# Pairs of tokens for k, a shorter end of MoE2, and a new written-out order in an attention and two-MoE kernel

## The chip, the cores and the metric

One core of one Trainium2 chip runs the whole program in one launch. The metric is the device time of one execution in microseconds (us). The kernel before ran three times: 928.71, 931.66 and 931.54 us, median 931.54. Durations are taken from one more execution, the profiled one.

## The reference

```python
scores = scale * np.matmul(q, k.transpose(0, 1, 3, 2))        # B, H, S, D = 4, 8, 576, 64
bias = -(cum[:, :, :, None] - cum[:, :, None, :])             # cum = cumsum of max(s, 0)
scores = np.where(causal, -1e9, scores + np.minimum(bias, 0.0))
attn = softmax(scores)
x = np.matmul(attn, v)                                        # to 2304 x 512
h = x @ moe_w_in                                              # 512 x 2048
x = (h - np.tanh(h)) @ moe_w_out
out = ((x @ moe2_w_a) * (x @ moe2_w_b)) @ moe2_w_out          # d_ff 1536
```

The inputs are fp32. The kernel makes most products from fp16 pieces: a value is a high and a low half, and a product takes three matmuls.

## The kernel before, in words

**Attention.** The work is cut into units, each a pair of heads of one batch (`Unit`, L968). A first-half unit has the first two tiles of 128 tokens as queries and two tiles of keys (`nk` = 2); a second-half unit (`merged`) has the rest. There are 16 of each. `g_load` (L993) loads q, k and v for a group of 2 or 4 units. A second-half group already reads the first two tiles of k and v as pairs of tokens: a row of 512 bytes holds tokens 2p and 2p+1, so that tile 0 has the even tokens and tile 1 the odd ones. For its queries all those keys are allowed, so their order does not matter. A first-half group reads each tile on its own, in rows of 256 bytes. `g_scale` and `split` scale q and k and cut them into fp16 halves (`qk`), `u_turn` (L1107) has the DMA queue transpose them to `qkT` and copies parts to `qB` and `kB`, whose extra rows hold the bias (`u_load`, from a DRAM buffer that `bias_parts`, L1796, fills). `u_qk` (L1139) then makes, for each head and query tile t, two matmuls over (t+1) x 128 key columns, and DVE adds the causal mask. Softmax, transposes and the product with v follow.

**MoE1 and MoE2.** Each block of tokens goes through MoE1 and MoE2. The last blocks use a scheme with seven products for four (`seven`, L1548, operands `ghl`), and the output product is treated in the same way (`four_act`, L1639, and `four_mm`, L1661, operands `sq`). `four_act` makes the operands of two halves of the tokens; those of the second half (l = 1) go to DRAM (`pb_d`) and are read back into a tile `x2f` when `four_mm` needs them. For the last two pieces of the last block's second half the output product is plain and sums up in two PSUM banks of its own, `blk["plain"]`. `four_out` (L1710) copies sums from PSUM (e into the one buffer "th", f into one of two "g"), combines them into `ob` and scales the rows by y1 and y2 (`out_rows`, L1729); `plain_out` (L1701) adds the plain sums, and `out_store` (L1738) issues the store, on SP or ACT for the last 512 rows.

**The order.** All operations are recorded first, so that the profile has one line, L647, for all of them, and an operation is told by its tiles. Then `emit` (L452) writes them out in the order that the string `ORDER` (L37) holds: three characters are one step, an operation's number and, where several engines may do it, the choice. `follow` (L445) uses the string if its length fits the number of operations. `cost` (L684) holds the durations by which a planner would set an order; with a fitting string it decides nothing. Tiles of a pool come free in this order too, so a tile with one buffer ties its users together.

```python
            for m, (qs, ks) in enumerate(u.pairs):
                pl.tensor.matmul(
                    pq[:, :n * P], qs[:, qat(u, h, t), :],
                    ks[:, h * u.wk:h * u.wk + n, :].rearrange("p a c -> p (a c)"),
                    start=(m == 0), stop=(m == 1))
```

Of the kernel before, what the change touches and what calls it, by code (L numbers as in the profile page):

```python
# [41 lines left out]
    "AFNAFgAMYAQIAGUAGgAQMAGkAKJAGoAHgAHkAG9APcAPkAYUAh0AHoAPsAGuAPgAH8AP0AGwAHAAHuAG0AZIAHEAh8AKBAHwAG5AHIAKQAKUAKYAKcAKgAH0"
    "AKkAJmAIAALQAFkAMuAM1AKoAQgALcAIEAP4AIIAYYAiQAKsAKyAM6AM8ALBAH5ALEAP8ALIAXwAK0ALgANIAJpALUALYALkANAARAANEAQwARQAlcAYcANM"
    "ANQALMAX0AX4AX8ALoAYgALsALyAK4AYAAK8AMBANUAYEAZQAL0AMEAIMANYANeAIRANtAN8AL4AL9AYIANwAOAAMIAiMAOIANhAUQAPoANkAYOAMMAiIAN0"
    "AYkAOEAjIAiUAOMAOQANpAiYAicAUYAikAigAOUAQkAN4AioAixAOYAMQAOeAOtAisAYoATwAOwAO0Ai9AOgAOkAQoAMVAlqAT4AO5AOoAO8AliAjAAQsAjV"
    "AjYAPAAlkAT8AT0AZcAjcAjMAjEAlsAl0AlxAUAAUEAQ0AYsAQ4AjRAUUAjgAZgAZkAi0AZoAYQAQ8ARgAZwAUcAUgAREAUkAUIAUMAUwAaAAZ0AYyAi4ARI"
    "An8AY0AZUARMAakAjlAaEAaIAU4AU8AjqAU0AVAAkgAj4ARwAjsAaMAaUAaYAZsAaoASgARVAoAAUsARYAjwAqSAj0Aj8AkAAl4Al8AasAksAn2AkkAawARl"
    "ARoARcAn4AZYAoIARsASAAqUAR1AkEAVEAkoAbIAqKAoGAZ4AUoAVQAVUAkwAR4AVYAVcAkIAk0AbMAbsASwAa4ASkAkMAnwAmAAmEAVMAVIAa8AZ8AR8AkU"
    "AbQAVgAqMAVwAk4AkQAadAmIAoNAk8AbwAagAbUAV4AbCAkYAb0AbYAcQASEAmMAV0AlIAlAAVkAmQAV8AWAASoAnAAnEAbcAmUAcUAcYASIAnIAqcAa0AoS"
    "AlFAzMAlMAbgAkcAbEAmYAb4AccASQAVsAmcAb8Am0AckAcAAqaAmgAm4Am8AcEAcoAlQAzYAS0AS4AblAzQAzUAzgAoUASMAboAc0AnMASUAmkAmpAoYAnQ"  # L50
    "AnUAcKAzcAWEAVoAcMAocAnYAlUAlYASYApIAc4AWMAndAmsAcuAc8AngAzkAdAAaQAqiApUA5MAdIApMAogApQAzoAdMAScAdYAWIAWQAmwAnkAWUAqmApY"
    "AokApcAooASsAdcAcwATAApgAdgAosAzsApkAS8ApoApxAowAdkAdQAptAWYAWcAzwAqoAqsAz0Ap0Ao8Ao2AdUApAAdsAWwAW4ATQAnoAntAp4Aq0AWgArc"
    "AdwAWkAW8Aq4Ad8AeAAqwAo5ApEAroAeEArgAegAd2Az4Ad4ATEAq8ArABEoAz8A0AArEAWoATIArQArKArsArwBEwArkAdoAekAeoAW0ATMAXAA0kArMAWs"
    "Ar0Ap8A0EAeIATUA0JAXEA0yAXIAr4AeQA0MA0qA24Ar8AsBAcgArUAsEATYAesA0YA28AXMAeUA3EAqAA0cATgAsIA00A0sATcAXQAXUAXYAXcAfoAfEAeZ"
    "A3IAecATlA3AA0gAToATsA3OA06AXgAsMArYA08AsQAsUAsYA5QAgMA5YAfsAfwAfIAdEAf0A0QA1EAewAfMAXkAscAf4AsgA3QAskA1CA3YAf8BE8AXsBEs"
    "AssA1IBE0A7kBE4AgQA7sA18Ae0AgwAfQAswAsoAfYA3UAs1As4A1UAtgAtoAtsAuIAe4Ag0A0UAtkAtBAgUAtFAfUAeMA1MAgYA5dAgcAtIA2AA1QAg4A1Y"
    "A5UAfcA2EA1cAg8As8A3cA5kA1gAgAA3oAe8A7wAtMAuMA1kAtQAhAA7oA1oAtUA3gBFQBFIAuQAtwA3sA1tAtZAhIAt0AXoAfAAggA3wAt4AfiA3kAt8AuU"
# [92 lines left out]
    "EXsEYQEVkEXZEXwEXcEYgEY0EY8EYkEXiEY5EZIEZMEbUEZQEYcEZUEbMEbcEbIEYVEYZEbYEZBEXkEZYEZ9EbQEbgEVoEZcEZlEZtEZxEZpEZhEZ0EZ4EaB"  # L150
    "EX4EX8EX0EbkEbsEboEbwEb0EaIEb4EaMEb8EaZEcAEaVEcsEcwEc0EaQEaEEc4Ec8EdAEacEahEapEasEakEa1Ea4EawEa8EbAEcEEcNEcIEcREcZEcgEcU"
    "EccEcoEdYEdcEdhEclEdIEdNEdQ"
# [1895 lines left out]
```

## Time and profile before

| | |
|---|---|
| median of three runs | 931.54 us |
| the profiled execution | 930.71 us |
| its span, first to last instruction | 928.9 us |
| PE, DVE, ACT, POOL busy | 881.3, 805.7, 574.1, 346.1 us |
| instructions | 20616 |
| moved by DMA | 123.38 MB |
| mean granted TensorE clock | 0.995 |

PE is the engine for matmuls, PEld its weight loads, DVE, ACT and POOL the vector, scalar and GpSimd engines; SP only issues DMAs (SPq, and ACTq for those that ACT issues). The busy times are sums over the whole span, for PE 95% of it. They don't tell in which stretch an engine waits, so the rows below come from windows and timelines.

### The profile page before, as it was taken

To read this page: it belongs to the slowest core of one execution; us is meant where nothing else is said; L and a number is where in the kernel's file an instruction comes from. 1 tells how busy PE (TensorE), PEld (TensorE's weight loads), DVE (VectorE), ACT (ScalarE), POOL (GpSimd) and SP (SyncE) were. 2 spreads that over 40 slices of the span, in tenths; PEclk is the share of its full clock that TensorE was granted. 3 is DMA by queue.
4 is the path that set the end of the run, shared out by engine and by line. 5 is a ranking of instruction groups with operands and counts; after the bars stand their busy time and mean duration, and the time that the engine had idled before them with its cause. 6 is when DMAs were issued, how large, how long until landed. Compare 5 with 4: busy or idle time off the path is not lost.

```text
span 928.9 us, 20616 instructions
## 1 busy us (share of the span) xinstructions
PE 881.3 (95%) x7650; PEld 647.6 (70%) x7650; DVE 805.7 (87%) x2011; ACT 574.1 (62%) x1136; POOL 346.1 (37%) x495
## 2 busy tenths in 40 slices
...
GB/s 204 304 214 238 231 123 124 113 154 171 206 165 174 193 179 167 208 137 161 308 206 189 84 24 1 69 2 1 47 54 53 60 185 65 62 72 112 72 68 115
DMA packets 260197, 123.38 MB, mean 133 GB/s; under 512 B 228544, under 2 KB 236976, under 8 KB 260096
## 3 DMA queue, kind: packets, MB, share of 16 engines
...
q8 instruction: 60, 0.98, 0.4%
q14 instruction: 41, 0.34, 0.1%
...
## 4 chain that ended last, share of the span: by engine, by line
PE 47%; DVE 5%; issue 2%; DMA 1%; POOL 1%; ACT 0%; SPq 0%; POOLq 0%; DVEq 0%; ACTq 0%
PE h L647 16%; PE qk L647 12%; PE acc L647 11%; PE pv L647 8%; DVE w L647 1%; DVE x2f L647 1%; DVE g L647 1%; DMA x2f<-pb_d 0%; DMA out_dram<-x2f 0%; DVE a L647 0%; DVE ghl L647 0%; DVE sq L647 0%; DVE xf L647 0%; DVE h L647 0%; DVE th L647 0%
## 5 line engine op out<-in xcount | busy, mean ns | idle before, releaser
L647 PEld LDWEIGHTS <-w 128*128 128x128 f16 x3840 | 372.2, 98 | 67.0 <-issue 4.0
L647 PE MATMUL h<-xhl,w 128*128 128x256 f16 x2256 | 276.9, 273 | 2.4 <-DVE ghl L647 1.1
L647 PE MATMUL acc<-w,ghl 128*128 128x512 f16 (+1 forms) x1092 | 233.6, 358 | 0.9 <-DVE sq L647 0.9
L647 PEld LDWEIGHTS <-ghl 128*128 128x128 f16 x1290 | 123.6, 98 | 99.9 <-issue 4.8
L647 PE MATMUL h<-xf,w 128*128 128x256 f16 (+1 forms) x416 | 71.3, 310 | 0.0
L647 DVE CUSTOM_DVE_ANT_0 qk<-qk,caus,cs 128x384 f32<-128x384 f32 (+3 forms) x120 | 64.9, 555 | 2.8 <-PE qk L647 1.4
L647 PE MATMUL qk<-xf,w 128*128 128x256 f16 x432 | 55.2, 273 | 0.8 <-DVE xf L647 0.6
L647 PE MATMUL pv<-xf,w 128*128 128x256 f16 x432 | 55.0, 273 | 0.0
L647 ACT ACTIVATE g<-h 128x512 f32<-128x512 f32 x40 | 23.4, 592 | 48.8 <-PE h L647 27.0
L647 ACT ACTIVATE w<-w 128x1024 f32<-128x1024 f32 (+1 forms) x45 | 50.9, 1156 | 1.4 <-DVE w L647 1.4
L647 ACT ACTIVATE th<-h,xc 128x512 f32<-128x512 f32 x64 | 43.7, 683 | 9.5 <-PE h L647 7.4
L647 PE MATMUL qk<-qkT 128*128 128x128 f16 (+4 forms) x168 | 45.7, 316 | 3.7 <-ACT zs L647 3.1
L647 PE MATMUL qk<-kB,qB 67*128 67x128 f16 (+4 forms) x168 | 45.3, 313 | 3.9 <-ACT zs L647 2.2
L647 PEld LDWEIGHTS <-v 128*64 128x64 f16 x1440 | 37.7, 113 | 12.8 <-issue 10.8
L647 PEld LDWEIGHTS <-x2f 128*128 128x128 f16 x360 | 35.1, 98 | 7.1 <-DMA x2f<-pb_d 0.8
L647 DVE SCALAR_TENSOR_TENSOR h<-h,xc,th 128x512 f32<-128x512 f32 x48 | 36.0, 751 | 1.6 <-ACT th L647 1.6
L647 ACT ACTIVATE zs<-qk,nm 128x128 f32<-128x128 f32 (+1 forms) x64 | 30.2, 472 | 11.2 <-DVE nm L647 9.4
L647 DVE SCALAR_TENSOR_TENSOR ghl<-h,xsg,ghl 128x512 f16<-128x512 f32 x48 | 35.8, 746 | 1.4 <-ACT ghl L647 0.9
L647 DVE SCALAR_TENSOR_TENSOR a<-qk,sm,a 128x512 f16<-128x512 f32 (+1 forms) x56 | 35.2, 630 | 1.4 <-ACT a L647 1.0
L647 ACT ACTIVATE qk<-qk,nm 128x512 f32<-128x512 f32 (+1 forms) x56 | 31.7, 566 | 7.4 <-DVE nm L647 5.4
L647 ACT ACTIVATE sq<-qk 128x512 f32<-128x512 f32 x22 | 13.1, 594 | 37.4 <-PE qk L647 35.0
L647 PE MATMUL pv<-aT,v 128*64 128x128 f16 x960 | 34.5, 225 | 1.3 <-DVE aT L647 0.8
...
## 6 DMA issues: line engine op xcount, KB each, us to landing
...
```

The source lines that it names most:

```text
L647: return getattr(getattr(plan.nc, name), what)(*[real(a) for a in args], **{k: real(a) for k, a in kw.items()})
```

## The change

Five things change.

1. `g_load`: a first-half group reads k as pairs of tokens, one DMA in rows of 512 bytes in place of two in rows of 256 (five k loads in place of ten). `bias_parts` lays the first half's bias out in the same way.
2. `u_qk`: a first-half unit's products read k by stepping between the two tiles, so that the columns of the result are in the order of tokens again. Neighbouring elements of the moving operand are 256 bytes apart. Number and size of the matmuls stay: 64 of 128 and 64 of 256 columns.
3. `four_act` and `four_mm`: the last piece of the last block stays in its tile `sq4`; the store to `pb_d` and the load from it are left out.
4. `four_out` for the last block's second half (`own`): e and f use a part of the weight tile `w1`, and the rows are scaled by a product yy of y1 and y2, on any of three engines.
5. `cost` has other DMA rates, and `ORDER` is another string, for 4562 steps in place of 4569.

```diff
@@ -35,121 +35,121 @@
 ORDER = (
-    "AAMAAEAB0AAIAAQAAUAAAAAYABsAB4ABoABwAAcAAgAAkAAsAAwAA0ABEABJABNABSAAoAA4AA8ABAABVABZABkACEACAAB8ACIACMACQACYAQQAIkACUACc"
...
+    "AAMABwAAIABsAB0AAAABkAAEABoAAQAAUACAAAYAB8AB4AAcAAgAAkAAsAAwAA0AQIABEABJABNABRAIgABUABYAAoAA4ACEACIACMAA8ACUAIcAIQABAACQ"
...
@@ -701,9 +701,9 @@
         size = {F32: 4, I32: 4}.get(main.dtype, 2)
         b = rows * count(main) * size
         if what == "dma_start_transpose":
-            return 650.0, 1600.0, b / 220.0
+            return 650.0, 1600.0, b / 242.0
         hold = 475.0 if b < 2e4 else 636.0 if b < 9e5 else 560.0
-        return hold, 910.0 if b < 1e6 else 2000.0, b / (180.0 if main.shape[-1] * size < 512 else 360.0)
+        return hold, 910.0 if b < 1e6 else 2000.0, b / (150.0 if main.shape[-1] * size < 512 else 360.0 if b >= 1e6 else 300.0)
     if eng == "tensor":
         lhs = rd[0]
         rate = 4.0 if lhs.dtype == F32 else 1.0
@@ -1013,6 +1013,11 @@
                 pl.sync.dma_start(
                     t.rearrange("p (h t) d -> p h (t d)", t=w)[:, :, 0:far * D],
                     heads[:, 0:far * P, :].rearrange("h (p t) d -> p h (t d)", t=far))
+            if nm == "k" and not u.merged:
+                pl.sync.dma_start(
+                    t.rearrange("p (h t) d -> p h (t d)", t=w),
+                    heads[:, 0:nt * P, :].rearrange("h (p t) d -> p h (t d)", t=nt))
+                far = nt
             for x in range(far, nt):
                 pl.sync.dma_start(
                     t.rearrange("p (h t) d -> p t h d", t=w)[:, x],
@@ -1143,10 +1148,11 @@
         pl.hold = (u.a[h],)
         with pl.group():
             for m, (qs, ks) in enumerate(u.pairs):
-                pl.tensor.matmul(
-                    pq[:, :n * P], qs[:, qat(u, h, t), :],
-                    ks[:, h * u.wk:h * u.wk + n, :].rearrange("p a c -> p (a c)"),
-                    start=(m == 0), stop=(m == 1))
+                o, r = pq[:, :n * P], ks[:, h * u.wk:h * u.wk + n, :].rearrange("p a c -> p (a c)")
+                if not u.merged:
+                    r = ks[:, h * u.wk:h * u.wk + u.nk, 0:n * P // u.nk].rearrange("p a c -> p c a")
+                    o = o.rearrange("p (c a) -> p c a", a=u.nk)
+                pl.tensor.matmul(o, qs[:, qat(u, h, t), :], r, start=(m == 0), stop=(m == 1))
         c = col(u, h, t)
         pl.vector.tensor_tensor_reduce(
             out=pq[:, :n * P], in0=pq[:, :n * P], in1=caus[:, (NT - t) * P:],
@@ -1655,6 +1661,8 @@
                 copy_scaled(o[:, 0, to], x, 1.0)
                 lo_part(o[:, 1, to], x, 1.0, o[:, 0, to])
             res.append(o)
+        if many(blk, c) == 4 and c == C2 - 1:
+            return res
         pl.sync.dma_start(pb_d[(blk["nth"] - FOUR) * C2 + c][:, 0:2 * many(blk, c) * P], t, writes=[("pb", blk["nth"], c)])
         return res
 
@@ -1666,7 +1674,7 @@
             else:
                 blk["acc", l] = accs(4)
         o = blk["p", c][l]
-        if l:
+        if l and not (plain(blk, c) and c == C2 - 1):
             t = new("moe", [P, 1024], I32, "x2f", 2, True).bitcast(F16)[:, 0:2 * many(blk, c) * P]
             pl.sync.dma_start(t, pb_d[(blk["nth"] - FOUR) * C2 + c][:, 0:2 * many(blk, c) * P], reads=[("pb", blk["nth"], c)])
             o = t.rearrange("p (h s n) -> p h s n", h=2, n=P)
@@ -1701,16 +1709,19 @@
     def plain_out(blk, ob):
         for i in (1, 0):
             g = blk["off"] // P + 3 - i
-            yy = new("moe", [P, 1], F32, "wac", 3)
-            small("tensor_tensor", out=yy, in0=y1[:, g:g + 1], in1=y2[:, g:g + 1], op=ALU.mult)
+            yy = blk["yy", i]
             r = ob[:, i * 512:(i + 1) * 512]
             pl.vector.scalar_tensor_tensor(out=r, in0=blk["plain"][i], scalar=yy, in1=r, op0=ALU.mult, op1=ALU.add)
             out_store(g, r)
 
     def four_out(blk, l):
         z, y1_, y2_, x = blk["acc", l]
-        e = new("moe", [P, 512], F32, "th", 1, True)
-        f = new("moe", [P, 512], F32, "g", 2, True)
+        own = l and plain(blk, C2 - 1)
+        if own:
+            e, f = [w1[:, 14, i * 512:(i + 1) * 512].bitcast(F32) for i in range(2)]
+        else:
+            e = new("moe", [P, 512], F32, "th", 1, True)
+            f = new("moe", [P, 512], F32, "g", 2, True)
         ob = new("moe", [P, 1024], I32, "x2f", 2, True).bitcast(F32)
         copy_scaled(e, z, 1.0, True)
         copy_scaled(f, y1_, 1.0, True)
@@ -1723,17 +1734,22 @@
         pl.vector.tensor_tensor(out=ob[:, 0:256], in0=x[:, 0:256], in1=e[:, 0:256], op=ALU.add)
         for i in (1, 0):
             r = ob[:, i * 512:(i + 1) * 512]
-            out_rows(blk["off"] // P + 2 * l + 1 - i, r, r, not (l and plain(blk, C2 - 1)))
+            if own:
+                g = blk["off"] // P + 3 - i
+                blk["yy", i] = new("moe", [P, 1], F32, "wac", 3)
+                small("tensor_tensor", out=blk["yy", i], in0=y1[:, g:g + 1], in1=y2[:, g:g + 1], op=ALU.mult)
+                copy_scaled(r, r, blk["yy", i])
+                continue
+            out_rows(blk["off"] // P + 2 * l + 1 - i, r, r)
         return ob
 
-    def out_rows(g, ob, src, store=True):
+    def out_rows(g, ob, src):
         kw = dict(out=ob, in0=src, scalar1=y1[:, g:g + 1], scalar2=y2[:, g:g + 1], op0=ALU.mult, op1=ALU.mult)
         if src is ob:
             small("tensor_scalar", **kw)
         else:
             pl.vector.tensor_scalar(**kw)
-        if store:
-            out_store(g, ob)
+        out_store(g, ob)
 
     def out_store(g, ob):
         for p0, n, row in where[g]:
@@ -1799,10 +1815,10 @@
         R = B * H
         d = x[:R, 0:w].bitcast(F32)
         x = x[:R, w:w + 3 * w // 2].bitcast(F16).rearrange("p (k w) -> p k w", k=3)
-        far = FAR * P if w == S else 0
+        far = FAR * P
         for o, c in ((d, cr[:, 0:w]),) if not far else (
                 (d[:, 0:far].rearrange("p (t c) -> p t c", t=FAR), cr[:, 0:far].rearrange("p (c t) -> p t c", t=FAR)),
-                (d[:, far:w], cr[:, far:w])):
+                (d[:, far:w], cr[:, far:w]))[:1 + (w > far)]:
             pl.vector.tensor_scalar(
                 out=o, in0=c, scalar1=cr[:, base:base + 1], scalar2=sig[:R], op0=ALU.subtract, op1=ALU.mult)
         for i in range(3):
```

Three places in the order of the instructions follow. The number at the end of a tile's name tells instances apart.

SP at the start, from the first MoE1 weights (w1) to the first two DMA transposes. Here ws is raw q, k and v of the second group of two units (the first group's loads are ahead), part0_d the bias in DRAM. Before:

```order
L647 DMA w1_0_154<-in_moe_w_in_dram 128x4x512
L647 DMA ws_1_156<-in_v_dram 128x4x64 x2
L647 DMA part0_d_71<-x2f_0_124 48x1x256
L647 DMA ws_1_156<-in_q_dram 128x4x64 x2
L647 DMA ws_1_156<-in_k_dram 128x4x64 x2
L647 DMA part0_d_71<-x2f_0_124 48x1x256
L647 DMA_TRANSPOSE qkT_0_200<-qk_0_165 128x8x128
L647 DMA_TRANSPOSE qkT_1_204<-qk_1_163 128x8x128
```

And now:

```order
L647 DMA w1_0_131<-in_moe_w_in_dram 128x4x512
L647 DMA ws_1_138<-in_v_dram 128x4x64 x2
L647 DMA ws_1_138<-in_q_dram 128x4x64
L647 DMA part0_d_71<-x2f_0_133 48x1x256
L647 DMA ws_1_138<-in_q_dram 128x4x64
L647 DMA ws_1_138<-in_k_dram 128x4x128
L647 DMA part0_d_71<-x2f_0_133 48x1x256
L647 DMA_TRANSPOSE qkT_0_190<-qk_0_170 128x8x128
L647 DMA_TRANSPOSE qkT_1_196<-qk_1_164 128x8x128
```

The group's two k loads are one, and the second tile of q is issued behind the first bias store.

DVE at the start, from the second bias step to the scaled sum of squares p2n (x2f: the bias here; icap and cap: limits of the scales). Before:

```order
L647 TENSOR_TENSOR x2f_0_124<-x2f_0_124 32x256
L647 TENSOR_SCALAR icap_0_129<-p2a_0_117 128x1
L647 TENSOR_SCALAR cap_0_131<-sig_0_121 128x1
L647 TENSOR_SCALAR icap_0_129<-icap_0_129 128x1
L647 TENSOR_SCALAR icap14_0_134<-icap_0_129 128x1
L647 TENSOR_TENSOR x2f_0_124<-x2f_0_124 32x256
L647 TENSOR_SCALAR x2f_0_124<-x2f_0_124 32x256
L647 TENSOR_SCALAR p2n_1_148<-pv_1_146 128x3
```

And now:

```order
L647 TENSOR_TENSOR x2f_0_133<-x2f_0_133 32x256
L647 TENSOR_SCALAR x2f_0_133<-x2f_0_133 32x256
L647 TENSOR_SCALAR icap_0_142<-p2a_0_124 128x1
L647 TENSOR_SCALAR cap_0_144<-sig_0_128 128x1
L647 TENSOR_SCALAR p2n_1_148<-pv_1_146 128x3
```

One TENSOR_TENSOR on the bias is gone from DVE here, and two of the four small steps come behind p2n.

DVE at the end, to its last instruction (x2f_26: the last block's first half; x2f_31: its second half; the last two rows add the plain products). Before:

```order
L647 TENSOR_TENSOR g_92_13063<-g_92_13063,th_92_13074 128x512
L647 TENSOR_TENSOR x2f_26_13117<-qk_222_12488,g_92_13063 128x512
L647 TENSOR_TENSOR x2f_26_13117<-qk_223_12489,th_92_13074 128x256
L647 TENSOR_SCALAR x2f_26_13117<-x2f_26_13117,y1_0_1749,y2_0_8637 128x512
L647 TENSOR_TENSOR th_93_13127<-th_93_13127 128x256
L647 TENSOR_TENSOR x2f_31_13132<-g_93_13130 128x256
L647 TENSOR_TENSOR g_93_13130<-g_93_13130,th_93_13127 128x512
L647 TENSOR_TENSOR x2f_31_13132<-qk_234_12955,th_93_13127 128x256
L647 TENSOR_TENSOR x2f_31_13132<-pv_142_12954,g_93_13130 128x512
L647 TENSOR_SCALAR x2f_31_13132<-x2f_31_13132,y1_0_1749,y2_0_8637 128x512
L647 SCALAR_TENSOR_TENSOR x2f_31_13132<-acc0_20_13085,wac_36_8639,x2f_31_13132 128x512
L647 SCALAR_TENSOR_TENSOR x2f_31_13132<-acc1_20_13078,wac_35_8641,x2f_31_13132 128x512
```

And now:

```order
L647 TENSOR_TENSOR th_92_13063<-th_92_13063 128x256
L647 TENSOR_TENSOR x2f_31_13084<-qk_234_12927,w1_0_131 128x256
L647 TENSOR_TENSOR x2f_31_13084<-x2f_31_13084,w1_0_131 128x256
L647 TENSOR_TENSOR x2f_31_13084<-pv_142_12926,w1_0_131 128x512
L647 TENSOR_TENSOR g_92_13066<-g_92_13066,th_92_13063 128x512
L647 TENSOR_TENSOR x2f_26_13109<-x2f_26_13109,th_92_13063 128x256
L647 TENSOR_TENSOR x2f_26_13109<-qk_222_12491,g_92_13066 128x512
L647 TENSOR_SCALAR x2f_26_13109<-x2f_26_13109,y1_0_1772,y2_0_8608 128x512
L647 TENSOR_TENSOR x2f_26_13109<-qk_223_12492,th_92_13063 128x256
L647 TENSOR_SCALAR x2f_26_13109<-x2f_26_13109,y1_0_1772,y2_0_8608 128x512
L647 SCALAR_TENSOR_TENSOR x2f_31_13084<-acc0_20_13070,wac_36_8877,x2f_31_13084 128x512
L647 SCALAR_TENSOR_TENSOR x2f_31_13084<-acc1_20_13077,wac_35_8677,x2f_31_13084 128x512
```

The four sums of x2f_31 have moved ahead of the last of x2f_26, and its scalings are gone from DVE, to ACT and POOL.

## Rows read from the trace of the kernel before

**Rows 1.** Stages: us, busy time of PE, PEld, DVE, ACT, POOL, PEclk, DMA share, GB/s

```profile
0.00:17.00 17.00, 0.49 (x3) 0.41 (x4) 12.91 (x47) 9.88 (x20) 3.29 (x13) 1.00 0.80 189
17.00:45.00 28.00, 19.41 (x144) 12.61 (x144) 26.32 (x113) 26.70 (x69) 14.95 (x28) 1.00 1.05 293
45.00:170.00 125.00, 118.61 (x801) 78.18 (x799) 120.63 (x388) 116.01 (x257) 51.54 (x94) 0.99 0.83 179
170.00:430.00 260.00, 257.66 (x2685) 170.46 (x2685) 234.86 (x657) 207.24 (x417) 124.43 (x174) 1.00 0.90 171
430.00:475.00 45.00, 41.17 (x349) 27.82 (x348) 41.03 (x96) 39.45 (x56) 9.91 (x14) 1.00 0.70 246
475.00:920.50 445.50, 444.00 (x3676) 358.15 (x3674) 365.87 (x710) 174.81 (x320) 140.49 (x171) 1.00 0.24 74
```

**Rows 2.** Timeline of the start: start, us busy, engine, line, operation, tiles

```profile
9.36 0.14 DVE L647 TENSOR_SCALAR p2n<-pv 128x3 f32<-128x3 f32 x1
...
10.78 0.88 DVE L647 SCALAR_TENSOR_TENSOR qk<-ws,sc,qk 128x256 f16<-128x256 f32 x2
...
11.43 1.05 SPq L647 DMA_DIRECT2D ws<-in_k_dram  x2
...
13.22 2.81 SPq L647 DMA_TRANSPOSE qkT<-qk  x2
...
17.38 0.27 PE L647 MATMUL qk<-qkT 128*128 128x128 f16 x1
```

**Rows 3.** Two windows of the start: rows of 256 bytes arrive, then long rows

```profile
2.00:5.00 3.00, 0.00 (x0) 0.00 (x0) 1.16 (x2) 0.00 (x0) 0.98 (x4) 1.00 0.92 198
7.00:9.00 2.00, 0.16 (x1) 0.00 (x0) 1.80 (x8) 1.45 (x6) 0.40 (x1) 1.00 1.03 376
```

**Rows 4.** PE timeline in 17 to 45, at 63 and at 150 us; qkT alone

```profile
18.40 0.42 PE L647 MATMUL acc<-qkT 128*128 128x256 f16 x1
...
18.61 0.42 PE L647 MATMUL acc<-kB,qB 67*128 67x256 f16 x1
...
63.33 3.62 PE L647 MATMUL h<-xf,w 128*128 128x256 f32 x16
...
150.39 0.27 PE L647 MATMUL qk<-qkT 128*128 128x256 f16 x1
...
150.50 0.27 PE L647 MATMUL qk<-kB,qB 67*128 67x256 f16 x1
...
17.00:45.00 28.00, 5.50 (x16) 2.19 (x16) 0.96 (x3) 1.23 (x2) 1.85 (x3) 1.00 1.05 293
```

**Rows 5.** Timeline of the end, and the group of scalings on DVE

```profile
908.65 0.69 DVE L647 SCALAR_TENSOR_TENSOR ghl<-xtail,ghl 128x512 f16<-128x512 f32 x1 [0.78 <-ACT ghl L647]
...
910.51 0.82 PE L647 MATMUL acc<-w,ghl 128*128 128x256 f16 x6
...
917.68 2.75 PE L647 MATMUL acc<-w,x2f 128*128 128x512 f16 x12
...
918.23 0.69 DVE L647 TENSOR_TENSOR x2f<-qk,g 128x512 f32<-128x512 f32 x1
...
918.84 0.41 DVE L647 TENSOR_TENSOR x2f<-qk,th 128x256 f32<-128x256 f32 x1
...
919.35 0.60 ACT L647 ACTIVATE th<-h 128x512 f32<-128x512 f32 x1 [10.73 <-DVE x2f L647]
...
923.24 0.75 DVE L647 SCALAR_TENSOR_TENSOR x2f<-acc,wac,x2f 128x512 f32<-128x512 f32 x1
...
923.38 0.77 POOL L647 TENSOR_SCALAR x2f<-x2f,y,y 128x512 f32<-128x512 f32 x1 [0.75 <-DVE x2f L647]
...
924.02 1.47 ACTq L647 DMA_DIRECT2D out_dram<-x2f  x2
...
924.19 0.75 DVE L647 SCALAR_TENSOR_TENSOR x2f<-acc,wac,x2f 128x512 f32<-128x512 f32 x1 [0.20 <-POOL x2f L647]
...
L647 DVE TENSOR_SCALAR x2f<-x2f,y,y 128x512 f32<-128x512 f32 x8 | 4.7, 585 | 0.3
```

More of the change, by code (lines that the diff above doesn't have):

```diff
@@ L42 @@
[L42 to L57, printed above, removed]
@@ L150 @@
[L150 to L152 removed]
+    "AAMABwAAIABsAB0AAAABkAAEABoAAQAAUACAAAYAB8AB4AAcAAgAAkAAsAAwAA0AQIABEABJABNABRAIgABUABYAAoAA4ACEACIACMAA8ACUAIcAIQABAACQ"
+    "ABgACYAFwACgACcACyAC9ADEAIUADIAIYACkAFoAQMAQQAIsAIkAF0ACsABcADAADQAIoAFsAC0AF8AIwAF5ADNAPAAQUAYwAO8APGAI0AI4AJAAY0ACoAI8"
@@ new lines @@
+    "ADUAJEAC4AP4ADZADcAEcADoAJIAFkAJwAJoAMUAMcAPJAh4AJ0ADgADkAJtAp4ADsADwAEoAJ8AY4AJMAEgAEkAMYAD0AD4APoAGAAEsAEwAJkAGGAENAEQ"
+    "AMhAMoAhoAh0AhwAHIAD8AEUAGUAPMAHMAE0AEAAE4AE+AFBAPQAY8AKGAFNAJYAFQAJQAGIAGYAGMAHQAFUAP8AEYAHUAFEAFZAFJAEEAQAAEIAFcAGQAHY"
+    "AGcAQEAGgAHcAKBAPUAGkAYMAMQAHgAG5AHkAH4AGqAGsAJ5AGwAKIAPsAG8AhsAHAAHqAHsAH8AJVAMyAQYAJeAG1AKMAHEAKUAKYAFhAKQAKcALUALIALM"
+    "AIAAMmALYAMtAKgAQ4AHwAH1AIEAPwAYQALQAKkAKqAPcAiEAZAAM0AN0AK5AP0AXoAKsAK8AKwALcAZEAYUAYYAZIAi8AM4AYgANAANEAM8AJhAXsAK0AXw"
@@ new lines @@
+    "AX0ANIALgALkAIIAL5ALAAX8ALqANMAL8AN4AMAANQAINANlALtAQoAYAANWAYcANZASYAiAALEAOAANoALwAL1AYGAMEAUIAOEANsANcANhAPYAh8AiIAiM"
+    "AN8AiQAiYAOIAOMAUQANwAQcAiUAicAilAOQAigAOlAjAAQgAX4AToAlQAMIAYkAOWAixARIAOoAOsAOYAOcAleAlWAOgAi0AMNATwAOxAllAPgAlYAQkAlg"
+    "AO0AO4ATsAloAjQAjJAT0Ai4AioAZUAZYAZcAjFAZgAZkAZoAT4AQsAQwAQ8AUUAT8AjMAjUAUMAYIAUYARAAUAAQ0ARYAUEAYpAUoAUwAnwAZ4AUcAitAZ8"
+    "AYsAZMAREAacAaAAaEAjeAU0AaMAZsAPkAUsAaQAjZAjgAU4AkUARNAn0ARQAjsAagAakAUkAjwAUgAnqARoAkYAj0AaoAjkAqGAawAkcAjoAlsARUAVIASo"
@@ new lines @@
+    "AbAARdAZQARgAlwAnsAn8ARtAU8ARwAkgAkkAn6AZwARkAR4AVQAVUAbkAqIAkoAj4AR0Aj8AkIAbEAbIAVAAl0AZ0AVEAoBAp8AqAAksAkAAkEAboAbsASc"
+    "Aa0ASIAVMAVYAbwAVoAVsAcIAaWAnkAVwAkMAkQAl4AmAAl8AkwAbMAbUAaYAa6Ak0Ak5Ak9ASgAmEAmIAzEAlAAqQAoGAVcAR8AV0Am0Am4Am8AV4AbQAcM"
+    "AbYASAAcQAlEAcUAmoAmMAmQAmUAmsAmwASMASsAzIAb0AVkAqOAccAb4AzABEcAoIAzQAa8Ab8ASEAnAAnEAcsAnIASwAbdAmYAbgAcCAmdAoMAoQAV8Acg"
+    "AnMAmgAnRAzMAqaAVgAcEAlIAlMASQAqUAcmAzYAzUAo8AcwAc0Ac4AnUAdAAdEAWEAasApIAnYAoUApAApEASUAdQApMAWAApQAWIAmkASkAoYAzcAS4AdU"
@@ new lines @@
+    "AdYApUApYApcAocAcoApkAS0AogAphAdIAokAoqATIAWQAowAWUAWMAWYAqcAdcAqgAqkAzgAzkAd0ApoApsAWoAWwAo0A48ArQAdMAaIAdkAeYAS8AncAnh"
+    "AdoAotAWcAduAW0Ao4Ad4Ad8A0UArUAqoAqsAqwArcAecAWgAzoAdwAq0AzsAzwAq4ATAAq+AWsAdgArYBEsArgAWkAegATEArEArAArkAz0AW4AroBEYAz5"
+    "AW8ApwATMA0iArsA0IArwAr4ATQAekA0aAeAA20Ar1Az8AcYAeIAXAAXEArIATYA0MA2sAeMAr8A0kAp0Ae8A0cAsAATUAXIAXQAXMArMAfgA0sAeRA24AeU"
+    "ATdATgA2wA0QBEkAXUAXYAsEAsIA3AAsMATkAfkA2+A0qA0yA5IAgEA5AAfoAXcAfAAfEAc8AsQA0AAeoA00AfsAsUAfwAXkA2oBEoAeEAsYAf0AgIA3IA04"
```

192 lines of the change are left out of this document (97 added, 95 removed).

## The prediction, made before the changed kernel ran

> **What bounds the kernel now.** I read the table of stages first, because the shares of the whole span (PE 95%) hide where PE still waits. [Rows 1] cut the span at the points where PE's work changes. In 475 to 920.5 us PE is busy 444.0 of 445.5 us, in 170 to 430 it is 257.7 of 260: nothing but less work on PE can shorten these. In 45 to 170 it is 118.6 of 125, with DVE (120.6) and ACT (116.0) nearly as full. PE stands still in four places only: before 17 us (16.5 us idle), in 17 to 45 (8.6), in 45 to 170 (6.4) and in 430 to 475 (3.8). After its last product at 920.5 come another 8.4 us of span, in which PE does nothing. So the time is a lead-in, a solid block of products, some gaps in the first 170 us, and a tail; I price the change in each.
>
> Second, the timeline of the start [rows 2]. The reader should follow one chain: p2n, the scaled sum of squares, is made on DVE at 9.36, behind steps for the bias; from p2n come the scales, from these the scaled fp16 pieces of q and k, the last piece of the first unit is there at 10.78 + 0.88 = 11.66, and yet its DMA transpose is issued by SP at 13.22, because SP is busy with the queue ahead of it (two k loads from 11.43, and a bias store behind them). The first score product runs at 17.38.
>
> Third, the timeline of the end [rows 5]. PE's last group of 12 products starts at 917.68 and ends at 920.43. But DVE is behind: it reads those accumulators only at 923.24 and 924.19 and ends at 924.94, which is 4.51 us after PE. From there to the end of the span (928.9) are 3.96 us of stores. The chain of waits agrees: it runs over PE almost everywhere and over DVE and the stores at the end.
>
> All sums are made against the profiled execution, 930.71 us (span 928.9 and 1.8 around it). That is 0.83 below the median of the three runs, 931.54; they lie between 928.71 and 931.66, so 0.3% (2.8 us) is about what can be told from no change.
>
> **The change, part by part.**
>
> *The end.* The change gives the second half's sums buffers of their own, so that four_out(1) need not wait for "th" and "g" to come free; the order shows its four DVE sums (x2f_31) ahead of four_out(0)'s last steps (x2f_26), where they stood behind before. In the profile ACT's first copy for it (th<-h) starts at 919.35 after 10.73 us of waiting for a buffer that DVE reads last [rows 5]; after the change it can start when its products end. What DVE has left when PE approaches its end T is: the two sums of four_out(0), 0.69 and 0.41, and their two scalings at 0.585 (the group of eight), 2.27 us in all. They wait for the last nine qk products. Behind these stand only the last 12 products, of 512 columns, which follow each other by twice the 0.11 of 256 columns [rows 4]: 12 x 0.22 = 2.6, so the wait ends at T - 2.6. DVE ends them at T - 0.3. Then come the two steps of 0.75 that add the plain products: they end at T + 0.45 and T + 1.2, in place of T + 4.51. The last two stores used to be shared by SP and ACT, and are now three on ACT and one on SP; ACT issues its two in 1.47 us [rows 5], so I add 0.5 us for the longer queue. Gain: 4.51 - 1.2 - 0.5 = 2.8; I take **-2.7**. Bounds: -3.3 (no added issue time) and -1.2 (ACT or POOL deliver the scaled half 1.5 us late, two of POOL's 0.77 steps).
>
> *A thinner cover before the end.* Nine qk products that stood before the last second-half products have moved behind them, so PE has about one microsecond less to do while the last operand of the sevenfold products (ghl) is made. In the profile that operand was ready at 908.65 + 0.69 = 909.34, its first product is at 910.51: 1.17 us to spare, less 9 x 0.11 = 1.0 [rows 4, 5]. It is just covered, and a chain in a new order can be a little longer; I take **+0.3** (0 to +0.8).
>
> *The start.* On SP one issue fewer stands ahead of the first transposes (five in place of six behind the last v load), and on DVE p2n has one bias step and two of the four small icap and cap steps less ahead of it. Against that, the first group's one k load of both tiles now lies ahead of its second v load, on which p2n also waits: 128 KB that came later before, which cost 0.34 us at the 376 GB/s of 7 to 9 us, or 0.65 us at the 198 GB/s of 2 to 5 us [rows 3]. An SP issue is about half a microsecond (two k loads: 1.05). I take **-0.2** (-0.8 to +0.5).
>
> *k in rows of 512 bytes.* Two more k loads of 256 KB fall in 17 to 45 us, where the DMA share is 1.05 [rows 1]. At 198 GB/s for rows of 256 bytes and 376 for long rows [rows 3], each could take 1.32 or 0.70 us; for both 1.2 us at most. But in this stage DVE is busy 26.3 and ACT 26.7 of 28 us, and these, not transfers, are what PE waits on there; so **0** (0 to -1.2). Between 45 and 170 the DMA share is 0.83 and loads run ahead: 0.
>
> *The stepped products.* 128 products now read k by stepping between two tiles, 256 bytes from each element to the next: 64 of 128 columns and 64 of 256, 24,576 columns. No row shows a stepped fp16 operand. Lower bound: nothing, as the columns are the same. Upper bound, the nearest row in which an operand is fed more slowly: fp32 products take 3.62/16 = 0.226 us per 256 columns, about twice the 0.11 of the contiguous fp16 ones (150.39 to 150.50) [rows 4]; 24,576/256 x 0.11 = 10.6 us for a doubling. A quarter of them lie in 17 to 45 us (16 of the 64 qkT products), where they are 0.21 us apart already (18.40 to 18.61, the 1.2 GHz level; at 150 us it is the 2.4 GHz level) and PE is idle 8.6 us: they are hidden. So three quarters, +7.9, at most. I take **0**, by the row that is the same product with the same columns, contiguous; this is the term I know least about.
>
> The Trainium skill ("Advanced Engine Details and Errata", Memory Cachelines) speaks against this part: SBUF is read in lines of 16 bytes, full speed wants at least two hits on a line, and a new line at each access costs a penalty, without saying how much for a matmul. No run here shows it so far; by that rule the sum would be that of the first rival below, 936.0, in place of 928.1.
>
> *The round trip through DRAM.* One store and one load of 256 KB less near the end: PE is idle 1.5 us in the whole of 475 to 920.5 [rows 1], so the load was hidden. 0. If it was not, the gain is part of that 1.5.
>
> *The rest of the new order.* On PE it is nearly the order of before; the planner's new rates act through the order alone. In 45 to 170 and 430 to 475 there are 10.2 us of gaps to win or lose. **0** (-1.5 to +1.5).
>
> Sum: -2.7 + 0.3 - 0.2 + 0 = -2.6, so 930.7 - 2.6 = **928.1**. Bounds of the small terms taken together give this case 925.5 to 930.5.
>
> **The rivals.**
>
> *Stepped reads feed PE at half rate.* For it: the fp32 rows show that a moving operand can be the limit, and no product of this kernel has neighbours 256 bytes apart so far. Against it: each of the two tiles is still read in order, and no byte more than before. Price: +7.9 on PE in 45 to 170 us, which nothing hides because PE is busy 118.6 of 125 there, though DVE (96% busy) would take over part of the bound. 928.1 + 7.9 = **936.0**, slower. The point from which it decides: the other terms are worth -2.6 against the profiled execution, so 33% of that doubling (0.036 us more on each 256 columns) uses them up, and from (934.3 - 928.1)/7.9 = 78% of it (0.086 us) the time is over the median by more than 0.3%.
>
> *The tail's gain is not realised.* If ACT or POOL, which make four_out(1)'s sums from products that end only some microseconds before T, come late, DVE, which takes its steps strictly in order, holds four_out(0) behind them; a POOL step of this size takes 0.77 [rows 5] and the chain has three. With the ghl operand late on PE as well (+0.8): -1.2 + 0.8 + 0 = about **930.3**, no change.
>
> *The new order closes gaps early.* SP's five issues less and DVE's reordered start bring the first products forward by an issue or two, and the shorter k loads let the units behind them start earlier: -0.8 at the start, -1.2 in 17 to 45, -1 in 45 to 170 on top of the tail: **925.3**, faster.
>
> That the change does not do what it says I leave out: the order shows k arriving as 128x4x128 pieces, the last products reading sq4 and the new place of four_out(1).
>
> **How the numbers follow.** Forecast 0.52, half-rate reads 0.24, tail lost 0.11, gaps closed 0.13. The forecast lies 0.37% below the median; of its 0.52, 0.30 falls below 928.75 and 0.22 within 0.3%. The tail case is "same". Of the half-rate case 0.19 is slower and 0.05 a milder slowing that stays within. Gaps closed is faster. So faster 0.30 + 0.13 = 0.43, same 0.22 + 0.11 + 0.05 = 0.38, slower 0.19. The range goes from 925.0 (under it lies a part of the last case) to 936.5, which takes in most of the half-rate case; about 0.2 stays outside.
>
> **What would show it.** Right at the end: DVE's last step ends about 1.2 us after PE's last product, not 4.5. Right in the stepped products: two of 256 columns after 45 us follow each other by 0.11 us; 0.21 is the half-rate case, and PE's busy time in 45 to 170 then grows by several microseconds. At the start: the first score product before 17.38. In the cover: no wait of PE for ghl in the last 15 us. The prediction is wrong if the block of products (17 to T) changes its length by more than 2 us, whatever the tail does, or if the stores after DVE's last step take longer than 4.5 us.

## The result, and the profile after

| | before | the change |
|---|---|---|
| median of five runs | 931.66 us (928.71 to 932.51) | 936.20 us (935.10 to 937.77) |
| the profiled execution | 930.71 us | 935.10 us |
| its span | 928.9 us | 933.3 us |
| PE, DVE, ACT, POOL busy | 881.3, 805.7, 574.1, 346.1 us | 890.5, 803.3, 573.4, 346.9 us |

The ratio is 1.0057, with a 95% interval from 1.0042 to 1.0073: 0.57% slower, where a small gain was forecast. Ratios in this document are taken over all runs of the two kernels, not as the quotient of the two medians (here 1.0049).

The stages of the changed kernel, in the columns of [rows 1]:

```profile
0.00:17.00 17.00, 0.49 (x3) 0.41 (x4) 12.59 (x47) 9.98 (x22) 4.41 (x14) 1.00 0.79 194
17.00:45.00 28.00, 20.13 (x148) 13.13 (x148) 26.13 (x114) 26.73 (x67) 15.52 (x30) 1.00 1.08 317
45.00:170.00 125.00, 119.43 (x751) 74.83 (x749) 117.33 (x369) 112.99 (x248) 46.19 (x83) 1.00 0.74 172
170.00:430.00 260.00, 256.87 (x2673) 169.52 (x2671) 235.62 (x675) 205.61 (x417) 121.63 (x176) 0.99 0.88 167
430.00:475.00 45.00, 41.87 (x357) 28.61 (x355) 36.56 (x88) 36.34 (x53) 13.96 (x17) 1.00 0.76 251
475.00:928.10 453.10, 451.77 (x3729) 363.21 (x3726) 374.24 (x738) 181.76 (x326) 145.15 (x172) 1.00 0.24 75
```

In 45 to 170 us PE is busy as long as before (119.4 us, 118.6 in [rows 1]), but with 751 products in place of 801, while DVE has become less busy (117.3, 120.6 before). The same work takes PE longer there, and DVE waits. The score products say why. PE's timeline, at 18 and at 151 us, against [rows 4]:

```profile
18.45 0.41 PE L647 MATMUL acc<-qkT 128*128 128x256 f16 x1
18.70 0.41 PE L647 MATMUL acc<-kB,qB 67*128 67x256 f16 x1
...
151.15 0.41 PE L647 MATMUL qk<-qkT 128*128 128x256 f16 x1
151.40 0.41 PE L647 MATMUL qk<-kB,qB 67*128 67x256 f16 x1
```

A stepped product of 256 columns is followed by the next after 0.25 us; the contiguous one was after 0.11. At 18 us it is also 0.25, where the contiguous one took 0.21. The granted clock reads 1.00 or 0.99 in both stages, but a contiguous product takes twice as long at 18 us as at 150, as it does at a granted clock of 0.50 (shown under e4); so 18 us is taken for the 1.2 GHz level. There the stepping costs little, and at the 2.4 GHz level the stepped product gains nothing from the clock. The groups by form, first of the kernel before, then of the change (busy us, mean ns of one):

```profile
L647 PE MATMUL qk<-qkT 128*128 128x128 f16 x48 | 11.1, 232 | 3.7 <-ACT zs L647 3.1 <-DVE aT L647 0.5
...
L647 PE MATMUL qk<-qkT 128*128 128x256 f16 x24 | 6.5, 273 | 0.0
```

```profile
L647 PE MATMUL qk<-qkT 128*128 128x128 f16 x48 | 12.6, 263 | 3.8 <-ACT zs L647 3.3 <-ACT aT L647 0.5
...
L647 PE MATMUL qk<-qkT 128*128 128x256 f16 x24 | 9.7, 405 | 0.0
```

With their twins on kB these groups are 9.6 us longer in all (1.5 + 3.2 here, 1.6 + 3.3 there), which is the whole growth of PE's busy time (9.2) and a little more.

The start answers to [rows 2]:

```profile
9.17 0.16 DVE L647 TENSOR_SCALAR p2n<-pv 128x3 f32<-128x3 f32 x1 [0.78 <-PE pv L647]
...
12.52 2.73 SPq L647 DMA_TRANSPOSE qkT<-qk  x2
...
17.06 0.28 PE L647 MATMUL qk<-qkT 128*128 128x128 f16 x1
```

The first product comes 0.32 us earlier. And the end to [rows 5]:

```profile
918.72 1.19 ACT L647 ACTIVATE w<-h 128x512 f32<-128x512 f32 x2 [3.71 <-PE h L647]
...
925.31 2.75 PE L647 MATMUL acc<-w,sq 128*128 128x512 f16 x12
...
927.04 0.55 DVE L647 TENSOR_SCALAR x2f<-x2f,y,y 128x512 f32<-128x512 f32 x1
927.50 1.42 DVE L647 SCALAR_TENSOR_TENSOR x2f<-acc,wac,x2f 128x512 f32<-128x512 f32 x2
928.28 2.12 ACTq L647 DMA_DIRECT2D out_dram<-x2f  x3
```

ACT's copies of four_out(1) wait for the products alone (<-PE h). PE ends at 928.06 and DVE at 928.92, 0.86 us behind in place of 4.51; then 4.4 us to the end of the span in place of 3.96. The end is 3.2 us shorter, but it comes 7.6 us later (PE's end went from 920.43 to 928.06). As the first product runs 0.3 us earlier, the block of products is 7.9 us longer; the prediction named 2 us as the sign that it is wrong.

### The profile page after: what moved, and what is told of

It reads as the page before. It is cut to its first block, busy times and chain, and to the rows that moved or that the text cites. A ratio compares the mean times of both kernels' runs of the same rounds, so it can differ in the third digit from the quotient of the medians.

```text
span 933.3 us, 20573 instructions
## 1 busy us (share of the span) xinstructions
PE 890.5 (95%) x7650; PEld 649.7 (70%) x7650; DVE 803.3 (86%) x2026; ACT 573.4 (61%) x1129; POOL 346.9 (37%) x490
## 4 chain that ended last, share of the span: by engine, by line
PE 53%; DVE 5%; issue 1%; DMA 1%; ACT 0%; POOL 0%; DVEq 0%; POOLq 0%; ACTq 0%
PE h L647 18%; PE acc L647 13%; PE qk L647 13%; PE pv L647 9%; DVE w L647 1%; DVE x2f L647 1%; DVE ghl L647 1%; DMA x2f<-pb_d 1%; DVE a L647 0%; DVE xf L647 0%; DVE h L647 0%; DVE qk L647 0%; DVE g L647 0%; DVE am L647 0%; DVE sq L647 0%
## 5 line engine op out<-in xcount | busy, mean ns | idle before, releaser
L647 PE MATMUL qk<-qkT 128*128 128x128 f16 (+4 forms) x168 | 51.1, 343 | 3.8 <-ACT zs L647 3.3
L647 PE MATMUL qk<-kB,qB 67*128 67x128 f16 (+4 forms) x168 | 50.9, 341 | 3.5 <-POOL qB L647 2.2
L647 ACT ACTIVATE g<-h 128x512 f32<-128x512 f32 x35 | 20.6, 592 | 33.0 <-PE h L647 24.4
L647 ACT ACTIVATE sq<-w 128x1024 bf16<-128x1024 f32 (+2 forms) x33 | 26.1, 797 | 23.0 <-DVE w L647 11.2
```

The source lines that it names most:

```text
L647: return getattr(getattr(plan.nc, name), what)(*[real(a) for a in args], **{k: real(a) for k, a in kw.items()})
```

## The experiments

Theory A: the stepped reads cost PE about 10 us, most of it on the path. Theory B: the stepping hides beside DVE, and the new order or the loads cost the time. The kernels e1 to e11 follow in the order of the argument.

**e1: contiguous reads, all else as changed.**

```diff
-                if not u.merged:
-                    r = ks[:, h * u.wk:h * u.wk + u.nk, 0:n * P // u.nk].rearrange("p a c -> p c a")
-                    o = o.rearrange("p (c a) -> p c a", a=u.nk)
```

> The changed kernel, but first-half products read their columns of k one after the other, so the keys stand in the order of pairs under a mask for the order of tokens (the scores of the first half are those of other keys). Loads, order and end of the change stay. Theory A (stepping costs PE: in the changed kernel 256 columns follow each other by 0.245 us in place of 0.11, about 10 us on PE after 45 us): spacing back to 0.11, PE busy about 880 us, time 926 to 929 (10 us less, of which DVE, 117 of 125 us busy in 45 to 170, may keep up to 3). Theory B (the new order or the loads made it slower, stepping is hidden beside DVE): spacing 0.11 as well, but the time stays within 1.5 us of 936.

Measured: 927.96 us, ratio to before 0.9977 (0.9963 to 0.9990). One access pattern taken out of 128 products gives 0.80% back, 7.4 us (8.2 between the medians, of which 1.0 is the kernel before, faster in this set of runs). Theory A.

**e2: runs in the read, steps in the write.**

```diff
-                    r = ks[:, h * u.wk:h * u.wk + u.nk, 0:n * P // u.nk].rearrange("p a c -> p c a")
-                    o = o.rearrange("p (c a) -> p c a", a=u.nk)
+                    r = ks[:, h * u.wk:h * u.wk + u.nk, 0:n * P // u.nk]
+                    o = o.rearrange("p (c a) -> p a c", a=u.nk)
```

> The changed kernel, but first-half products read k in runs (tile 0, then tile 1) and write the result in steps of two columns, so that the result is in the order of tokens again. If the cost sits in reading a new place of SBUF for each column: spacing 0.11 us per 256 columns and the time of e1, 926 to 929. If writing every other fp32 column of PSUM costs as much: spacing 0.2 or more and 934 to 938. The Trainium skill (Advanced Engine Details and Errata, Memory Cachelines) says of PSUM that lines hold two fp32 values and that matmuls slow down where neighbours are not side by side, which speaks for the second.

Measured: 936.07 us, ratio 1.0053 (1.0039 to 1.0067). PE's timeline:

```profile
141.77 0.42 PE L647 MATMUL qk<-qkT 128*128 128x256 f16 x1
141.99 0.42 PE L647 MATMUL qk<-kB,qB 67*128 67x256 f16 x1
```

0.22 us: here writing every other fp32 column of PSUM is nearly as dear as the stepped read, and the whole kernel takes as long. So the cost can't be moved to the other side of the product. The Trainium skill says so of PSUM ("Advanced Engine Details and Errata", Memory Cachelines: lines of two fp32 values, and matmuls slow down where neighbours are not side by side), and the trace agrees.

It is another limit, though. In 116 to 117 us of this execution the granted clock was 0.50, and there the products are 0.43 us apart:

```profile
116.45 0.71 PE L647 MATMUL qk<-qkT 128*128 128x256 f16 x1
116.88 0.71 PE L647 MATMUL qk<-kB,qB 67*128 67x256 f16 x1
```

The stepped write takes twice the time at half the clock. The stepped read does not, as e4 shows.

**e3: the new order and the new end, without the long rows and the stepping.** Contiguous products as in e1, bias in the order of tokens, and k by tiles:

```diff
+                with pl.group():
+                    for x in range(nt):
+                        pl.sync.dma_start(
+                            t.rearrange("p (h t) d -> p t h d", t=w)[:, x],
+                            heads[:, x * P:(x + 1) * P, :].rearrange("h p d -> p h d"))
```

> The changed kernel with k loaded tile by tile in rows of 256 bytes as before (two DMAs at the place of one), bias in the order of tokens, products contiguous: the new order and the new end alone. If the pair loads are worth nothing (DVE and ACT bound the stage): the time of e1 within 0.7 us. If transfers bound 17 to 45 us: up to 1.2 us over e1, with the gap in that stage. Against before: 3 to 6 us faster (the end is 3.2 shorter in the trace of the changed kernel).

Measured: 929.22 us, ratio 0.9983 (0.9973 to 0.9992). Against e1 the rows of 512 bytes are worth 0.06%, less than the intervals. The gain on before is only 1.4 us, under the 3 to 6 expected: something in this kernel seems to give back half of what the end gained.

**e4: the kernel before, with nothing but the stepping added** (the three lines of e1, put in).

> The kernel before with one thing changed: first-half products read k by stepping between its two tiles (the keys of the result then stand in a mixed order). Theory A: spacing 0.245 us after 45 us, PE busy 881 to 891, time 931.7 + 8 to 10 = 940 to 942. Theory B (hidden beside DVE): within 1.5 us of 931.7.

Measured: 938.11 us, ratio 1.0081 (1.0068 to 1.0094), 7.5 us over before; two products are 0.24 us apart:

```profile
143.15 0.41 PE L647 MATMUL qk<-qkT 128*128 128x256 f16 x1
143.39 0.41 PE L647 MATMUL qk<-kB,qB 67*128 67x256 f16 x1
```

Theory A again, a little under the 8 to 10 expected.

e4 also shows what the clock does to the stepped read. In one stretch of it the granted clock fell to 0.50, the 1.2 GHz level, with stepped products inside; in e1 contiguous products met the same. First e4, then e1 (the last row of each is a window, with PEclk as its third number from the end):

```profile
89.78 0.41 PE L647 MATMUL qk<-kB,qB 67*128 67x256 f16 x1
90.03 0.41 PE L647 MATMUL qk<-qkT 128*128 128x256 f16 x1
...
89.50:90.50 1.00, 1.00 (x5) 0.60 (x4) 0.85 (x2) 1.00 (x3) 0.26 (x1) 0.50 1.80 198
```

```profile
112.53 0.42 PE L647 MATMUL qk<-qkT 128*128 128x256 f16 x1
112.75 0.42 PE L647 MATMUL qk<-kB,qB 67*128 67x256 f16 x1
...
112.00:113.00 1.00, 1.00 (x7) 0.58 (x6) 0.96 (x2) 0.99 (x3) 0.00 (x0) 0.50 0.43 96
```

At a granted clock of 0.50 stepped products are 0.25 us apart and contiguous ones 0.22; at 1.00 it is 0.24 to 0.25 and 0.11. The stepped read has a limit of its own that does not go with PE's clock.

**e5: the new end alone.** The kernel before with the edits of four_act, four_mm, four_out, plain_out and out_rows in the diff above, and its own order up to about 800 us; from there the changed kernel's steps.

> The kernel before with the new end alone: no round trip for the last piece, four_out of the second half with buffers of its own, and the changed kernel's order for the last tenth of the steps (from about 800 us); loads, products and order ahead of that are those of before. If the end is worth what the traces show (DVE's last step 0.87 us behind PE's last product in place of 4.51, stores 0.4 longer): PE's end at 920 to 921 us as before and 930.7 - 3.2 = 927.5. Rival (the new end makes the block of products before it longer, as in e3, where PE ends 2.5 us later than before): PE's end at 922 to 923 and 929 to 930.

Measured: 926.67 us, ratio 0.9964 (0.9952 to 0.9976). PE's and DVE's last rows:

```profile
916.98 2.75 PE L647 MATMUL acc<-w,sq 128*128 128x512 f16 x12
...
919.19 1.42 DVE L647 SCALAR_TENSOR_TENSOR x2f<-acc,wac,x2f 128x512 f32<-128x512 f32 x2
```

PE ends at 919.73, not later than before, DVE 0.88 us after it. The end is worth 3.4 us, and what e3 lost is put down to the new order ahead of it: 0.9983 - 0.9964, or 1.8 us. The two intervals just touch, so this is an estimate and not a clear difference.

**e9: where the new order loses.** e5, with the changed kernel's steps in the string from about 350 us on.

> e5 with the changed kernel's order from about 350 us on, in place of about 800. In e3 and in e1, which have the whole new order, PE waits 2.1 us at 388 us for a sum of squares, because ACT's copy of the last attention sums (xf<-pv) waits 2.05 us for DVE (xtail); in e5 there is no such wait. If the 2.5 us that e3 is slower than e5 come mostly from there: a wait of about 2 us at 388 us and e5 + 1.4 to 2 = 928.1 to 928.7. If they come from the first 350 us: 926.7 within 0.5, and no such wait, or one that is won back.

Measured: 927.50 us, ratio 0.9974 (0.9960 to 0.9988): 0.1% over e5, half of what e3 lost. The wait is there, first in e9, then the same place in e5:

```profile
384.71 0.47 ACT L647 ACTIVATE xf<-pv,inv 128x256 f32<-128x256 f32 x1 [2.05 <-DVE xtail L647]
...
386.42 0.16 PE L647 MATMUL pv<-xmx,ones 128*128 128x1 bf16 x1 [2.07 <-ACT sq L647]
```

```profile
383.56 0.47 ACT L647 ACTIVATE xf<-pv,inv 128x256 f32<-128x256 f32 x1
...
385.67 0.18 PE L647 MATMUL pv<-xmx,ones 128*128 128x1 bf16 x1 [0.19 <-DVE xtail L647]
```

The stall came with the order, as expected, but less of it reached the end than 1.4 us, and the intervals of e5, e9 and e3 overlap. How the 1.8 us divide over the two parts stays open.

The clock is a reason not to read such a difference from single profiles. Behind some of PE's waits the granted clock falls to 0.50 for a few microseconds, and each time 1.7 us of products are lost. It is not the same in every execution: in the profile of the changed kernel the clock falls behind this very wait (0.50 in 394 to 397 us, the wait of 2.07 us ends at 392.98), in those of e3 and e9 it does not. e9's profile has no such stretch at all, e5's has one, behind a wait at 79 us that e9 has too. So e9's profiled time (926.65 us, e5's 926.61) does not show the stall to be free, and what the wait costs on average was not measured.

**e6: how long must a run be?** Runs of 2, 4 and 8 columns by batch, in one execution:

```diff
+                    e = (8, 2, 4, 8)[u.b]
+                    r = r.rearrange("p a (c e) -> p c a e", e=e)
+                    o = o.rearrange("p (c a e) -> p c a e", a=u.nk, e=e)
```

> The changed kernel, with first-half products reading k in runs: 2 columns of tile 0, then 2 of tile 1 for batch 1, runs of 4 for batch 2, of 8 for batches 0 and 3 (the keys then stand in another order than the mask). If every change of place costs the same (0.135 us for 256 changes): 256 columns follow each other by 0.18, 0.145 and 0.13 us for runs of 2, 4 and 8. If it is enough that two neighbours lie side by side: 0.12 or less already for runs of 2. The Trainium skill (Advanced Engine Details and Errata, Memory Cachelines) asks for two hits on a line, which is the second.

Measured, in order of time runs of 2, of 4 and of 8:

```profile
58.23 0.30 PE L647 MATMUL qk<-qkT 128*128 128x256 f16 x1
58.37 0.30 PE L647 MATMUL qk<-kB,qB 67*128 67x256 f16 x1
...
114.23 0.28 PE L647 MATMUL qk<-qkT 128*128 128x256 f16 x1
114.35 0.28 PE L647 MATMUL qk<-kB,qB 67*128 67x256 f16 x1
...
150.69 0.27 PE L647 MATMUL qk<-qkT 128*128 128x256 f16 x1
150.80 0.27 PE L647 MATMUL qk<-kB,qB 67*128 67x256 f16 x1
```

0.14, 0.12 and 0.11 us. The cost does not fall with the number of changes (that would be 0.18 for runs of 2): two neighbours side by side remove about four fifths of it. By the Trainium skill's rule of two hits on a line ("Advanced Engine Details and Errata", Memory Cachelines) it would be all of it; the trace says nearly.

**e11: distance or neighbourhood?** Every e-th element of a stretch, in one execution:

```diff
+                    z = ks[:, 0:2 * u.wk, :].rearrange("p a c -> p (a c)")
+                    e = (1, 2, 4, 2)[u.b] if not t else (1, 2, 2, 1)[u.b]
+                    r = z[:, 0:n * P * e].rearrange("p (c e) -> p c e", e=e)[:, :, 0]
```

> The changed kernel with other columns read in the first half's products (the scores are then not those of the reference): batch 1 every second fp16 element of one stretch, batch 2 every fourth in the 128-column products and every second in the 256-column ones, batch 3 every second in the 128-column ones. If what costs is that the neighbour of a column is not the next element: 256 columns 0.24 us apart at a stride of 2 already, as with 256 bytes. If it is the distance (a place that was just read is free): 0.11 to 0.14 at strides of 2 and 4, as with runs of 2 in e6.

Measured, a stride of 2 elements with 256 columns, then a stride of 4 with 128:

```profile
84.42 0.28 PE L647 MATMUL qk<-qkT 128*128 128x256 f16 x1
84.54 0.28 PE L647 MATMUL qk<-kB,qB 67*128 67x256 f16 x1
...
116.62 0.28 PE L647 MATMUL qk<-qkT 128*128 128x128 f16 x1
116.72 0.30 PE L647 MATMUL qk<-kB,qB 67*128 67x128 f16 x1
116.84 0.29 PE L647 MATMUL qk<-qkT 128*128 128x256 f16 x1
```

A stride of 2 costs next to nothing (0.12 for 256 columns, and 0.06 for 128 at 149 us). A stride of 4, 8 bytes from element to element, makes 0.10 to 0.12 of 0.06, almost as much as the 256 bytes of the changed kernel (0.12 for 128 columns, at 153 us). So it is not that the next element is skipped: with e6, what counts is whether near neighbours are taken together, and 8 bytes are already too far. How many bytes come at once was not measured.

**e7: long rows, runs of 64.** A tile's even tokens stand ahead of its odd ones, in k's columns, in the mask and in v's rows:

```diff
+                    r = ks[:, h * u.wk:h * u.wk + u.nk, 0:n * P // u.nk].rearrange("p a (g c) -> p g a c", g=n)
+                    o = o.rearrange("p (g a c) -> p g a c", g=n, a=u.nk)
...
+                        for y in range(2):
+                            pl.sync.dma_start(
+                                t.rearrange("p (h t) d -> p t h d", t=w)[y * 64:y * 64 + 64, x],
+                                heads[:, x * P:(x + 1) * P, :].rearrange("h (p y) d -> y p h d", y=2)[y])
```

> The changed kernel with k still in rows of 512 bytes, but first-half products read k in runs of 64 columns, so that within a tile of keys the even tokens stand ahead of the odd ones; v is loaded in that order of rows (two DMAs of 64 partitions each) and the mask has it too. Nothing is left out. If runs of 64 cost nothing and v's split loads neither: spacing 0.11 and the time of e1, 927.3 to 928.6. If v's loads in halves cost what k's pair loads gained: 929 to 930, the time of e3.

Measured: 931.92 us, ratio 1.0012 (1.0001 to 1.0024), worse than both guesses. The products are 0.11 us apart again, but the start has paid:

```profile
6.35 3.20 SPq L647 DMA_DIRECT2D ws<-in_v_dram  x4
...
14.41 2.74 SPq L647 DMA_TRANSPOSE qkT<-qk  x2
...
18.49 0.27 PE L647 MATMUL qk<-qkT 128*128 128x128 f16 x1
```

Four more v loads for the first two groups hold SP, which issues everything in order; the transposes go out at 14.41 (12.52 in the changed kernel), the first product runs at 18.49 (17.06).

**e8: the same in the order of before**, k in two DMAs by halves of the heads.

> The kernel before, in its order, with k in rows of 512 bytes (two DMAs by halves of the heads, at the places of the two by tiles) and products in runs of 64 as in e7. If pair loads are worth 1.3 us (e1 against e3): 929.4. If that was the new order's or noise: 930.7 within 0.7.

Measured: 931.62 us, ratio 1.0016 (1.0004 to 1.0028): no gain, for the same reason:

```profile
15.69 2.75 SPq L647 DMA_TRANSPOSE qkT<-qk  x2
...
19.47 0.27 PE L647 MATMUL qk<-qkT 128*128 128x128 f16 x1
```

Transposes and first product come 2.5 and 2.1 us later than in [rows 2].

**e10: each cost where it is cheap.** e5, with k in long rows; the first block steps (PE is idle there, and [rows 4] have it at 0.21 anyway), the later blocks use the runs of e7, with mask and v to match:

```diff
+                if not u.merged and u.j:
+                    r = ks[:, h * u.wk:h * u.wk + u.nk, 0:n * P // u.nk].rearrange("p a (g c) -> p g a c", g=n)
+                    o = o.rearrange("p (g a c) -> p g a c", g=n, a=u.nk)
+                elif not u.merged:
+                    r = ks[:, h * u.wk:h * u.wk + u.nk, 0:n * P // u.nk].rearrange("p a c -> p c a")
+                    o = o.rearrange("p (c a) -> p c a", a=u.nk)
```

> e5 (order of before, new end) with k in rows of 512 bytes (two DMAs by halves of the heads), made as cheap as it can be: the first block's products step between the tiles, where PE is idle anyway (16 of 64 pairs, ahead of 45 us), the later blocks read runs of 64 with v's rows loaded to match (two DMAs of 64 partitions for each tile). Nothing is left out. If the long rows are worth something once the stepping is gone: 925.5 to 926.4. If they are hidden and v's six more issues cost nothing either: 926.7 within 0.4. If the issues cost as in e7: 927.5 to 928.5.

Measured: 925.28 us, ratio 0.9942 (0.9929 to 0.9954). It beats both kernels: 0.58% under before, 1.14% under the change, and a little better than expected. It is 0.22% under e5, whose interval it touches, so long rows are worth between nothing and a few tenths of a per cent here; in the new order (e1 against e3) no gain could be told.

## Why the prediction was wrong

The runs make a chain from before to the change, one part at a time: before 1; with the new end 0.9964 (e5); with the new order too 0.9983 (e3); with the long rows 0.9977 (e1); with the stepped products 1.0057. The parts are -0.36, +0.19, -0.06 and +0.80%, or, of 931 us, -3.4, +1.8, -0.6 and +7.4 us.

- **The stepped products: the step that failed.** I took 0, "by the row that is the same product with the same columns, contiguous", and named it the term I knew least about. That row is nearest in everything but the one thing that the edit changes. Measured: 0.25 us for 256 columns against 0.11, 9.6 us of PE time, +0.80% of the whole. The upper bound from the fp32 rows (0.226) was close and a little low, and that is luck: those products go with the clock, and the stepped ones do not. In the kernel before four fp32 products took 1.71 us, 0.43 each, where contiguous fp16 ones are 0.21 apart (39.14 to 39.35):

```profile
39.57 1.92 PE L647 MATMUL h<-xf,w 128*128 128x256 f32 x4
41.28 0.42 PE L647 MATMUL qk<-eyeh,a 128*128 128x128 f16 x2
```

- **The first rival was what happened.** It gave 936.0, and 936.2 was measured, its spacing of 0.21 was 0.25, and the stage it named (45 to 170 us) is where PE lost. Some 2 us of the 9.6 did not reach the end (7.4 by the ratios). In the profiles PE waits less elsewhere: its idle time ahead of its end (that time less its busy time) is 928.1 - 890.5 = 37.6 us in the changed kernel and 923.0 - 882.2 = 40.8 in e1. That the sum met to 0.2 us is partly luck: the end gained more, the order lost something, and the sum starts from the profiled execution (930.71), almost 1 us below the median of before (931.66).
- **The rule.** The Trainium skill ("Advanced Engine Details and Errata", Memory Cachelines) names a penalty for a new line at each access, without a size; the 936.0 was the rival's price. The trace agrees that there is one: 0.25 us in place of 0.11. It does not agree that two hits on a line of 16 bytes are enough: a stride of 4 fp16 elements takes two from each line and still costs (e11).
- **The end: right.** -2.7 was forecast, -3.4 came (e5). DVE ends 0.86 us after PE, 1.2 was said; the longer queue of stores costs 0.4, 0.5 was said.
- **The thinner cover: not needed.** +0.3 was taken; PE has no wait for ghl in the last 15 us.
- **The start: right.** The first product is 0.32 us earlier, 0.2 was said.
- **Long rows at 0: right in this order**, as e1 and e3 can't be told apart.
- **The rest of the order at 0 (-1.5 to +1.5): too kind.** It costs about 1.8 us (e3 against e5, with intervals that touch); one piece of it may be the wait at 388 us, which my view of the order's two ends could not show.
- **The round trip at 0**: not tried by itself; it is part of e5.
- **The bounds.** The ends of the small terms' ranges add up to 923.9 and 932.3; the 925.5 and 930.5 of the prediction are narrower, and it does not show how they come about.

The chances followed the wrong pick: with 0 and +7.9 as the bounds of one term, and a rule that spoke for the upper one, 0.24 for that case was too little.
